# Turning the normalised rows of a fused attention and gated-MLP block: from DMA transposes to a layout in DRAM and VectorE transposes

## The chip, the cores and the metric

The kernel runs on one core of a Trainium2 chip. The metric is device time in microseconds (us) of one execution; three unprofiled runs of the kernel before gave 310.79, 310.81 and 311.08. One further execution was profiled, and the profile and the trace are from that one.

The core's engines each work through their own list of instructions in order: TensorE (PE in the profile; its weight loads are PEld), VectorE (DVE), ScalarE (ACT), GpSimd (POOL), and SyncE (SP), which here does nothing but issue DMAs. An instruction that waits holds up everything behind it on its engine. DMAs issued by SP run on 16 DMA engines.

## The reference: what is computed

```python
x = A_x                                   # 1 x 2048 x 640, bf16
xn = _layernorm(x)
return x + _A_ref(xn, A_wqkv, A_wo) + _B_ref(xn, B_w_gate, B_w_up, B_w_down)

def _A_ref(x, wqkv, wo):                  # 32 heads of 20, window 256
    q, k, v = (x @ wqkv)...               # reshaped to heads
    scores = q k^T * 20 ** -0.5           # causal, only the last 256 keys
    return softmax(scores) v @ wo

def _B_ref(x, w_gate, w_up, w_down):      # 640 -> 1536 -> 640
    return (sigmoid(x @ w_gate) * (x @ w_up)) @ w_down
```

## The kernel before

**Chunks and stages.** The 2048 rows are cut into four chunks (0 to 3) of 512 rows, four blocks of 128 rows each. Every product needs the normalised rows turned, features on the partitions: the tile `xnT[c]` (128 partitions, 5 feature groups, 512 rows). A chunk goes through these stages:

- normalising (`g_norms`, L366): for each block the statistics (`ln_block`: two BN_STATS and one aggregate on VectorE), then 1/sqrt of the variance for all four blocks on GpSimd (`rstd_blocks`, L284), then subtract and multiply on VectorE (`norm_block`, L290, tile `xn`), then the turn (`turn_block`, L302): a DMA transpose from SBUF to SBUF on SP's queue, `xn` into `xnT[c]`. Chunk 0 is turned by TensorE instead (`transpose_rows`, L296).
- `g_qk` (L391): ten products for queries and keys. Each is copied from PSUM into a staging tile `st` (six buffers; VectorE copies the queries at L323, ScalarE the keys at L325) and stored to a scratch tensor in DRAM, `sq` or `sk` (L327). From there `spread` (L329) loads the tiles `qT` and `kT` with heads of 20 padded to 32 rows. The pad rows are cleared once by DMA (`clear`, L196). The scratch exists twice, for even and odd chunks; the second pair is cleared by `clear_next`.
- `g_v` (L410): the values; each block gives two products `pv`, copied to the tile `v` by VectorE and ScalarE in turn (L358).
- `g_gu` (L432): gate and up products `pg`, `pu`; ScalarE takes tanh of `pg` (L439), and VectorE multiplies it with `pu` into `h` (L447). This `h` is 12 tiles per chunk.
- `scores` (L505) and `pv` (L531): scores of one step into `ps`, the exponential on ScalarE (`pT`, L517), masks on GpSimd (L524) or, for the steps called late, one mask on VectorE (L529), then `acc`. VectorE transposes `acc` to `t` (L555) and divides (`rec` L563, `on` L567, `oc` L571).
- `g_out` (L488): `y` from `h` and `wd` (L457) and from `oc` and `wo` (L464), the residual rows added by VectorE (L468) and the store.

`pqk`, `pv`, `pg`, `pu`, `acc` and `y` share four PSUM accumulators (pool `ps_d`): a product starts only when the copy out of the tile that had its accumulator is done.

**What sets the order.** The order is written out. The attention steps of all chunks stand in one list (`todo`). Between them the planner `Fill` (L574) draws products from a list of parts (L712 to L730), as many nanoseconds of them as a step leaves free; the cost of a part is fixed in the code. `mix(a, b, first, every, rest)` (L618) weaves two generators: after the piece of `a` with number `first`, and after every `every`-th from there, one piece of `b` follows. That is how the normalising of the next chunk gets in among the products of the current one: chunk 1 among the gate and up products of chunk 0 (`gu0a`, `gu0b`), chunk 2 in the output of chunk 0 (`out0`), chunk 3 in `gu1b` and `out1`. Loads are parts of cost 0.

**SP's queue** takes, after the parts for chunk 0: the transposes of chunk 1, the rows of chunk 2 (L159), the rearranging of the output weights from DRAM to DRAM (`turn_wo`, L229, tensor `wo_i`, eight transfers), `wd` (L225), the two pad clears (L198), four query stores, the output weights out of `wo_i` (`load_wo`, L235), and the rest of the stores and spreads. SP uses eight semaphores in turn for its DMAs, so a DMA is issued only when the one eight places earlier has landed.

## Time and profile before

| | |
|---|---|
| median of 3 unprofiled runs | 310.81 us (310.79 to 311.08) |
| profiled execution | 312.31 us |
| its span, first to last instruction | 310.5 us |
| granted TensorE clock | 1.0 |
| DMA | 35.67 MB in 40459 packets, 10560 of them under 512 B |
| transposes by DMA (L303) | 12, SP busy 1.2 us with one (median 1.22) |
| normalising, one block of 128x640 (L292) | 12, mean 640 ns |
| statistics, one half block (L272) | 28, mean 472 ns |
| VectorE transpose 128x512 bf16 (L571) | 20, mean 711 ns |

How to read the profile: a group of instructions has its line, engine, operation and tiles (out<-in), a count, and busy time. A line of the timeline starts with its start and its length in us, and ends, in brackets, with how long the engine had been idle before it and what ended that. In the list of waits, "A <- B: 2.0, 1, 2.0" is: A's engine waited for B, in total us, times, longest us. The chain that ended last is followed back from the last instruction through what released each step. "SPq" is SP issuing DMAs; when a DMA has landed is told by its semaphore in the trace.

### The profile page before, as it was taken

The page shows a single profiled execution, that of the slowest core. Times are in us where ns is not written, and L with a number is a line of the kernel's source. Part 1 is how long each engine was busy: PE and PEld are TensorE (multiplying, and loading weights), DVE is VectorE, ACT ScalarE, POOL GpSimd, SP SyncE. Part 2 cuts the span into 40 slices and gives each one's busy share as a digit, 9 for nine tenths or more (in the row PEclk, how much of TensorE's full clock was granted, in tenths as well). Part 3 has the DMA queues.
Part 4 walks back from the last instruction along what each step waited for, and adds up shares of the span by engine and source line. Part 5 has one row for each costly group of instructions (what it writes and reads, how often), then busy time and mean ns, then how long its engine had stood idle before and what let it go on. Part 6 is the DMA issues. An engine that isn't in the chain of part 4 may idle for free.

```text
span 310.5 us, 10034 instructions
## 1 busy us (share of the span) xinstructions
PE 302.4 (97%) x4343; PEld 168.1 (54%) x4343; DVE 172.0 (55%) x342; ACT 198.4 (64%) x196; POOL 165.3 (53%) x304
## 2 busy tenths in 40 slices
PE   6999999998999999999989999999999999999996
PEld 3654444544657654554556665454546665444774
DVE  5633684828697464496945346373643626372533
ACT  6923868668964648888654548978675647778000
POOL 3020668457885828566661836747383756657000
PEclk9999999999999999999999999999999999999999
DMA  7997984985705453440013512640000210000201
GB/s 206 365 327 237 330 155 150 344 260 165 231 0 89 108 158 121 155 160 2 3 23 88 87 56 89 211 155 1 4 0 4 67 40 23 2 2 2 87 23 63
DMA packets 40459, 35.67 MB, mean 115 GB/s; under 512 B 10560, under 2 KB 39872, under 8 KB 40384
## 3 DMA queue, kind: packets, MB, share of 16 engines
q1 hardware_dynamic: 39552, 34.27, 37.2%
q10 hardware_dynamic: 864, 0.77, 0.9%
q8 instruction: 34, 0.56, 0.8%
q14 instruction: 9, 0.07, 0.1%
HBM read 23.63 MB, written 10.26 MB: 109 GB/s over the span
## 4 chain that ended last, share of the span: by engine, by line
PE 90%; DVE 4%; DMA 2%; ACT 2%; issue 1%; SPq 0%; DVEq 0%; ACTq 0%
PE y L457 17%; PE pu L443 17%; PE pg L436 16%; PE pqk L319 12%; PE ps L512 8%; PE pv L349 7%; PE y L464 7%; PE acc L543 6%; DMA sq<-st 1%; ACT pT L517 1%; DVE on L567 1%; DMA xc<-in_A_x_dram 1%; DVE st L323 1%; DVE xn L292 1%; DVE h L447 0%
## 5 line engine op out<-in xcount | busy, mean ns | idle before, releaser
L524 POOL TENSOR_SCALAR_AFFINE_SELECT pT<-pT 64x512 bf16<-64x512 bf16 (+1 forms) x252 | 153.6, 609 | 103.6 <-ACT pT L517 91.8
L517 ACT ACTIVATE pT<-ps 128x2048 bf16<-128x2048 f32 x75 | 140.8, 1877 | 60.4 <-PE ps L512 57.5
L447 DVE SCALAR_TENSOR_TENSOR h<-th,pu 128x512 bf16<-128x512 f32 x48 | 32.8, 683 | 54.3 <-PE pu L443 41.7
L443 PE MATMUL pu<-xnT,wu 128*128 128x512 bf16 x240 | 59.8, 380 | 0.0
L436 PE MATMUL pg<-xnT,wg 128*128 128x512 bf16 x240 | 59.8, 380 | 0.0
L457 PE MATMUL y<-wd,h 128*128 128x320 bf16 (+2 forms) x396 | 56.8, 295 | 0.8 <-DVE h L447 0.8
L319 PE MATMUL pqk<-xnT,wqkv 128*128 128x512 bf16 x200 | 46.0, 381 | 0.0
L457 PEld LDWEIGHTS <-h 128*128 128x128 bf16 x396 | 36.6, 98 | 17.0 <-issue 2.2
L439 ACT ACTIVATE th<-pg 128x512 f32<-128x512 f32 x48 | 28.6, 596 | 15.3 <-PE pg L436 15.1
L436 PEld LDWEIGHTS <-wg 128*128 128x128 bf16 x240 | 22.3, 98 | 25.6 <-issue 2.0
L443 PEld LDWEIGHTS <-wu 128*128 128x128 bf16 x240 | 22.1, 98 | 25.4 <-issue 1.8
L319 PEld LDWEIGHTS <-wqkv 128*128 128x128 bf16 x200 | 22.6, 119 | 18.8 <-issue 1.4
L512 PE MATMUL ps<-qT,kT 20*64 20x320 bf16 (+4 forms) x1456 | 32.2, 259 | 0.3 <-issue 0.2
L512 PEld LDWEIGHTS <-kT 20*64 20x64 bf16 x1456 | 15.9, 103 | 24.8 <-issue 21.8
L555 DVE STREAM_TRANSPOSE t<-acc 128x512 f32<-128x512 f32 x32 | 21.1, 696 | 13.3 <-PE acc L543 13.3
L567 DVE TENSOR_TENSOR on<-t,rec 128x320 bf16<-128x320 f32 (+4 forms) x48 | 27.7, 576 | 1.1
L468 DVE SCALAR_TENSOR_TENSOR rows<-y,rows 128x320 bf16<-128x320 f32 x30 | 14.4, 488 | 23.8 <-PE y L464 23.5
L349 PE MATMUL pv<-wqkv,xnT 128*128 128x320 bf16 x160 | 25.9, 300 | 0.0
L464 PE MATMUL y<-wo,oc 128*128 128x320 bf16 (+2 forms) x165 | 24.2, 295 | 0.0
L543 PE MATMUL acc<-pT,v 64*32 64x320 bf16 (+4 forms) x1456 | 19.8, 252 | 1.4 <-DVE pT L529 1.4
L358 DVE CAST v<-pv 64x320 bf16<-64x320 f32 x29 | 14.1, 487 | 12.2 <-PE pv L349 11.9
L543 PEld LDWEIGHTS <-v 64*32 64x32 bf16 x1456 | 16.3, 91 | 7.4 <-issue 2.6
(48 smaller groups left out, 157.3 us busy)
## 6 DMA issues: line engine op xcount, KB each, us to landing
qT<-sq SPq DMA_DIRECT2D x16, 256.0 KB
kT<-sk SPq DMA_DIRECT2D x16, 256.0 KB
sq<-st SPq DMA_DIRECT2D x20, 128.0 KB
sk<-st SPq DMA_DIRECT2D x20, 128.0 KB
out_dram<-rows SPq DMA_DIRECT2D x15, 160.0 KB
wg<-in_B_w_gate_dram SPq DMA_DIRECT2D x4, 480.0 KB
wu<-in_B_w_up_dram SPq DMA_DIRECT2D x4, 480.0 KB
xc<-in_A_x_dram SPq DMA_DIRECT2D x3, 640.0 KB
```

The costliest lines, as they stand in the source:

```text
L319: nc.tensor.matmul(ps, lhsT=wt[:, m, :], rhs=xnT[c][:, d, :], start=(d == 0), stop=(d == DC - 1))
L349: nc.tensor.matmul(ps[:, 0:HALF], lhsT=xnT[c][:, d, s * P:(s + 1) * P], rhs=wqkv[:, d, 2 * D + hf * HALF:2 * D + (hf + 1) * HALF], start=( ...
L436: nc.tensor.matmul(pg, lhsT=part(wg, d, f), rhs=xnT[c][:, d, :], start=(d == 0), stop=(d == DC - 1))
L443: nc.tensor.matmul(pu, lhsT=part(wu, d, f), rhs=xnT[c][:, d, :], start=(d == 0), stop=(d == DC - 1))
L447: nc.vector.scalar_tensor_tensor(out=h, in0=th, scalar=1.0, in1=pu, op0=ADD, op1=MULT)
L457: nc.tensor.matmul(y[:, 0:cut[1] - cut[0]], lhsT=ht[c, f][:, s * P:(s + 1) * P], rhs=wd[:, f, cut[0]:cut[1]], start=(f == 0), stop=False)
L464: nc.tensor.matmul(y[:, 0:cut[1] - cut[0]], lhsT=oc[c, m][:, s * P:(s + 1) * P], rhs=wo[:, m, cut[0]:cut[1]], start=False, stop=(m == DC - 1))
L512: nc.tensor.matmul(ps[a * U:(a + 1) * U, i, col * U:(col + n) * U], lhsT=qk["k", kc, o // GH][32 * i:32 * i + DH, o % GH + a, kb * U:(kb + ...
L517: nc.scalar.activation(out=pt[:, :, 0:CW], in_=ps, func=EXP, scale=SCALE)
L524: nc.gpsimd.affine_select(out=view, in_=view, pattern=[[0, HG], [0, n], [sign, U]], compare_op=GE, fill=0.0, base=base, channel_multiplier ...
L543: nc.tensor.matmul(acc[32 * i:32 * i + 32, q * U:(q + n) * U], lhsT=vt[kb][a * U:(a + 1) * U, u, h * VW:h * VW + 32], rhs=pt[a * U:(a + 1) ...
L567: nc.vector.tensor_tensor(out=on[m][:, :, slot:slot + n], in0=t1[:, :, first:first + n], in1=rec.to_broadcast([P, 16, n]), op=MULT)
```

## The change

The rows of chunks 1 to 3 are no longer transposed by DMA. Each normalised block is stored to DRAM (`store_rows`, tensor `xr`, two of them). When all four blocks are stored, four loads (`load_quarters`) bring the chunk back so that quadrant q of 32 partitions holds columns 160q to 160q+159, and row t of each group of 32 rows lies on partition t; the tile is the one that held the raw rows (`xc`, one buffer). VectorE then transposes 32x32 blocks of it into `xnT[c]`, one instruction of 128x640 for a block of rows. Feature 5p+b thereby lands on partition p in group b, where before it was feature 128b+p on partition p; so `wqkv`, `wg` and `wu` are loaded by the same order, and chunk 0's TensorE transposes read every fifth column.

The statistics of chunk 1 start three pieces earlier in `gu0a`; those of chunk 2 move from `out0` into `v1` and those of chunk 3 from `gu1b` into `v2`; a number of empty pieces (`wait`) lies between the loads of the quarters and the transposes. The scratch tensors exist once and are cleared once. `turn_wo` is two transfers where it was eight, `load_wo` moves ahead of the rows of chunk 2, and these go behind `wd`.

```diff
-    wqkv_r = A_wqkv.rearrange("(c p) n -> p c n", p=P)
+    def by_feature(w):
+        return w.rearrange("(p b) n -> p b n", b=DC)
+    wqkv_r = by_feature(A_wqkv)
...
-    scratch = {(w, k): tc.dram_tile([H * 32, CW], BF16, name=f"s{w}{k}")
-               for w in "qk" for k in range(2)}
+    scratch = {w: tc.dram_tile([H * 32, CW], BF16, name=f"s{w}") for w in "qk"}
+    xn_rows = [tc.dram_tile([CW, D], BF16, name=f"xr{k}") for k in range(2)]
...
     def turn_wo():
-        for i in range(HG):
-            for a in range(2):
-                nc.sync.dma_start(out=wo_i[i].rearrange("(b a d) n -> a b d n", a=2, d=DH)[a],
-                                  in_=A_wo.rearrange("(a b i d) n -> i a b d n", a=2, i=HG, d=DH)[i, a])
+        for a in range(2):
+            nc.sync.dma_start(out=wo_i.rearrange("i (b a d) n -> a b i (d n)", a=2, d=DH)[a],
+                              in_=A_wo.rearrange("(a b i d) n -> a b i (d n)", a=2, i=HG, d=DH)[a])
...
     def transpose_rows(s, copy, lo=0, hi=DC):
+        xn = xns[0, s].rearrange("p (f b) -> p b f", b=DC)
         for d in range(lo, hi):
-            nc.tensor.transpose(pt[:, d, :], xns[0, s][:, d * P:(d + 1) * P], ident)
+            nc.tensor.transpose(pt[:, d, :], xn[:, d], ident)
...
+    def store_rows(c, s):
+        nc.sync.dma_start(out=xn_rows[c % 2][s * P:(s + 1) * P, :], in_=xns.pop((c, s)))
+    def load_quarters(c):
+        t = xp.tile([P, SBC, D], BF16, name="xc")
+        xc[c] = t
+        for q in range(4):
+            nc.sync.dma_start(out=t[32 * q:32 * q + 32].rearrange("p s (j e) -> p (s j) e", e=QF),
+                              in_=xn_rows[c % 2][:, q * QF:(q + 1) * QF].rearrange("(j t) e -> t j e", t=32))
     def turn_block(c, s):
-        nc.sync.dma_start(out=xnT[c][:, :, s * P:(s + 1) * P], in_=xns.pop((c, s)), transpose=True)
+        nc.vector.transpose(out=xnT[c][:, :, s * P:(s + 1) * P],
+                            in_=xc[c][:, s, :].rearrange("p (j f b) -> p b j f", j=SBC, b=DC))
...
         for s in range(SBC):
             norm_block(c, s, mvs[:, s, :], rstds[:, s:s + 1])
+            store_rows(c, s)
+            if s < SBC - 1:
+                yield 0
+        load_quarters(c)
+        for _ in range(wait):
             yield 0
-            if turn:
-                turn_block(c, s)
+        new_xnT(c)
+        for s in range(SBC):
+            turn_block(c, s)
+            yield 0
...
-    fill.add("gu0a", mix(g_gu(0, 0, 4), norms1, 4, 1, False), 4 * GU)
-    fill.add("gu0b", mix(g_gu(0, 4, 12), norms1, 0), 8 * GU)
-    fill.add("x2", later(load_x, 2), 0)
+    norms = {c: g_norms(c, wait) for c, wait in ((1, 8), (2, 7), (3, 7))}
+    fill.add("gu0a", mix(g_gu(0, 0, 4), norms[1], 1, 1, False), 4 * GU)
+    fill.add("gu0b", mix(g_gu(0, 4, 12), norms[1], 0), 8 * GU)
     fill.add("wo_i", later(turn_wo), 0)
     fill.add("wd", later(load_wd), 0)
-    fill.add("pads", later(clear_next), 0)
+    fill.add("wo", later(load_wo), 0)
+    fill.add("x2", later(load_x, 2), 0)
     fill.add("qk1", g_qk(1), 50 * MM)
-    fill.add("v1", mix(g_v(1), g_gu(1, 0, 2), 1, 2), 40 * 136 + 2 * GU)
-    fill.add("out0", mix(g_out(0, g_gu(1, 2, 3)), norms2, 1, 1), OUT + GU)
+    fill.add("v1", mix(mix(g_v(1), g_gu(1, 0, 2), 1, 2), norms[2], 2, 1, False), 40 * 136 + 2 * GU)
+    fill.add("out0", mix(g_out(0, g_gu(1, 2, 3)), norms[2], 1, 1), OUT + GU)
     fill.add("x3", later(load_x, 3), 0)
     fill.add("qk2", g_qk(2), 50 * MM)
-    fill.add("v2", mix(g_v(2), g_gu(1, 3, 7), 0, 1), 40 * 136 + 4 * GU)
-    fill.add("gu1b", mix(g_gu(1, 7, 12), norms3, 0, 1, False), 5 * GU)
-    fill.add("out1", mix(g_out(1, g_gu(2, 0, 1)), itertools.chain(norms3, g_turns(3)), 1, 3), OUT + GU)
+    fill.add("v2", mix(mix(g_v(2), g_gu(1, 3, 7), 0, 1), norms[3], 8, 1, False), 40 * 136 + 4 * GU)
+    fill.add("gu1b", mix(g_gu(1, 7, 12), norms[3], 0, 1, False), 5 * GU)
+    fill.add("out1", mix(g_out(1, g_gu(2, 0, 1)), norms[3], 1, 1), OUT + GU)
```

More of the change, by code (lines that the diff above doesn't have):

```diff
@@ L27 @@
 FS = 768
+QF = D // 4
 EPS = 1e-5
@@ L189, with clear @@
     load_wqkv(1)
-    scratch = {(w, k): tc.dram_tile([H * 32, CW], BF16, name=f"s{w}{k}")
-               for w in "qk" for k in range(2)}
+    scratch = {w: tc.dram_tile([H * 32, CW], BF16, name=f"s{w}") for w in "qk"}
+    xn_rows = [tc.dram_tile([CW, D], BF16, name=f"xr{k}") for k in range(2)]
     zero = kp.tile([P, GH, CW], BF16, name="kT")
     nc.gpsimd.memset(zero[:, 0:3, :], 0.0)
-    def clear(w, k):
-        rows = scratch[w, k].rearrange("(h j) s -> h (j s)", j=32)[:, DH * CW:]
+    def clear(w):
+        rows = scratch[w].rearrange("(h j) s -> h (j s)", j=32)[:, DH * CW:]
         nc.sync.dma_start(out=rows.rearrange("h (a e) -> h a e", a=4), in_=zero[:, 0:3, :])
@@ L201, in load_gu @@
         nc.sync.dma_start(out=t[k][:, :, lo:hi],
-                          in_=w.rearrange("(c p) f -> p c f", p=P)[:, :, k * FS + lo:k * FS + hi])
+                          in_=by_feature(w)[:, :, k * FS + lo:k * FS + hi])
     load_gu(wg, B_w_gate, 0, 0, FS // 2)
     load_gu(wu, B_w_up, 0, 0, FS // 2)
-    clear("q", 0)
-    clear("k", 0)
+    clear("q")
+    clear("k")
     load_gu(wg, B_w_gate, 0, FS // 2)
@@ L216, in load_rest @@
         spread("k", 0, 4, NG)
-    def clear_next():
-        clear("q", 1)
-        clear("k", 1)
     def load_wd():
@@ L325, in proj_block @@
             nc.scalar.copy(out=st, in_=ps)
-        dst = scratch[w, c % 2].rearrange("(h j) s -> h j s", j=32)
+        dst = scratch[w].rearrange("(h j) s -> h j s", j=32)
         nc.sync.dma_start(out=dst[:, 4 * m:4 * m + 4, :], in_=st)
@@ L333, in spread @@
             qk[w, c, half] = (qp if w == "q" else kp).tile([P, GH, CW], BF16, name=w + "T")
-        src = scratch[w, c % 2].rearrange("(a b p) s -> b p a s", a=2, p=P)
+        src = scratch[w].rearrange("(a b p) s -> b p a s", a=2, p=P)
         for b in range(g0 // 2, g1 // 2):
@@ L364, with g_norms @@
     MM = 216
-    def g_norms(c, turn, behind=0):
-        new_xnT(c)
+    def g_norms(c, wait):
         mvs = lnp.tile([P, SBC, nc.vector.BN_AGGR_DIM], FP32, name="mvs", bufs=1)
@@ L374, in g_norms @@
                 yield 0
-        for _ in range(behind):
-            yield 0
         rstds = rstd_blocks(mvs)
@@ L381, in g_norms @@
             norm_block(c, s, mvs[:, s, :], rstds[:, s:s + 1])
+            store_rows(c, s)
[3 more added lines that the diff above has]
+        for _ in range(wait):
             yield 0
-            if turn:
-                turn_block(c, s)
-    def g_turns(c):
+        new_xnT(c)
         for s in range(SBC):
@@ L398, in g_qk @@
                     load_gu(wu, B_w_up, 0, FS // 2)
-                if c == 1 and w == "q" and m == 3:
-                    load_wo()
                 if c and w == "k" and m == 1:
@@ L707, in later @@
         yield 0
-    norms1 = g_norms(1, True)
-    norms2 = g_norms(2, True, 1)
-    norms3 = g_norms(3, False)
-    fill.add("gu0a", mix(g_gu(0, 0, 4), norms1, 4, 1, False), 4 * GU)
-    fill.add("gu0b", mix(g_gu(0, 4, 12), norms1, 0), 8 * GU)
-    fill.add("x2", later(load_x, 2), 0)
+    norms = {c: g_norms(c, wait) for c, wait in ((1, 8), (2, 7), (3, 7))}
+    fill.add("gu0a", mix(g_gu(0, 0, 4), norms[1], 1, 1, False), 4 * GU)
+    fill.add("gu0b", mix(g_gu(0, 4, 12), norms[1], 0), 8 * GU)
     fill.add("wo_i", later(turn_wo), 0)
     fill.add("wd", later(load_wd), 0)
-    fill.add("pads", later(clear_next), 0)
+    fill.add("wo", later(load_wo), 0)
+    fill.add("x2", later(load_x, 2), 0)
     fill.add("qk1", g_qk(1), 50 * MM)
-    fill.add("v1", mix(g_v(1), g_gu(1, 0, 2), 1, 2), 40 * 136 + 2 * GU)
-    fill.add("out0", mix(g_out(0, g_gu(1, 2, 3)), norms2, 1, 1), OUT + GU)
+    fill.add("v1", mix(mix(g_v(1), g_gu(1, 0, 2), 1, 2), norms[2], 2, 1, False), 40 * 136 + 2 * GU)
+    fill.add("out0", mix(g_out(0, g_gu(1, 2, 3)), norms[2], 1, 1), OUT + GU)
     fill.add("x3", later(load_x, 3), 0)
     fill.add("qk2", g_qk(2), 50 * MM)
-    fill.add("v2", mix(g_v(2), g_gu(1, 3, 7), 0, 1), 40 * 136 + 4 * GU)
-    fill.add("gu1b", mix(g_gu(1, 7, 12), norms3, 0, 1, False), 5 * GU)
-    fill.add("out1", mix(g_out(1, g_gu(2, 0, 1)), itertools.chain(norms3, g_turns(3)), 1, 3), OUT + GU)
+    fill.add("v2", mix(mix(g_v(2), g_gu(1, 3, 7), 0, 1), norms[3], 8, 1, False), 40 * 136 + 4 * GU)
+    fill.add("gu1b", mix(g_gu(1, 7, 12), norms[3], 0, 1, False), 5 * GU)
+    fill.add("out1", mix(g_out(1, g_gu(2, 0, 1)), norms[3], 1, 1), OUT + GU)
     fill.add("qk3", g_qk(3), 50 * MM)
```

## The prediction

> **What bounds the kernel now.** I read the engine totals first, then the chain that ended last, then the waits.

> ```profile
> PE 302.4 (97%) x4343; PEld 168.1 (54%) x4343; DVE 172.0 (55%) x342; ACT 198.4 (64%) x196; POOL 165.3 (53%) x304
> ...
> PE 90%; DVE 4%; DMA 2%; ACT 2%; issue 1%; SPq 0%; DVEq 0%; ACTq 0%
> ```

> TensorE (PE) is busy 302.4 of 310.5 us and 90% of the chain is its own work. The order of its instructions, and ScalarE's, is the same in the changed program as built. So the change can only remove idle time of TensorE or add some. The table of 10 us stretches puts the idle at the start (2.4 us up to 10 us), at the end (3.6), and in between at 60-80 us (0.57 + 0.87), 150-160 (0.84) and some 0.3 more. The last three, about 2.6 us, are all that a better order could win. Who waits there, from the list of waits:

> ```profile
> ACT st L325 <- DMA sq<-st: 2.0, 1, 2.0
> ...
> PE acc L543 <- DVE pT L529: 1.4, 1, 1.4
> ...
> PE y L457 <- DVE h L447: 0.8, 1, 0.8
> ```

> The first two are one event, at 69.4-70.9 us; the chain in order of time shows it:

> ```profile
> 63.68 4.43 DMA sq<-st
> 68.14 1.90 ACT pT L517
> 70.14 0.69 DVE pT L529
> ```

> ScalarE may not overwrite a staging tile until its store to DRAM has landed. The first query store of chunk 1 was issued at 60.02 and landed at 67.02 (the trace's landings): on most DMA engines by 63.1, on four of them 3.9 us later. Those four still had the rearranging of the output weights (wo_i, L232): eight transfers of 4 rows of 25.6 KB, each landing on 4 engines. The DMA share while little else ran says so too:

> ```profile
> 51.00:52.00 1.00, 1.00 (x7) 0.43 (x5) 0.00 (x0) 1.00 (x2) 0.91 (x2) 1.00 0.19 77
> 52.00:53.00 1.00, 1.00 (x6) 0.45 (x5) 0.39 (x1) 0.57 (x2) 0.78 (x2) 1.00 0.27 111
> ```

> The two last columns, DMA share and GB/s: a fifth to a quarter is 4 of 16 engines.

> **The change, part by part**, in the clock of before.

> *Removed*: 12 DMA transposes (SP is busy 1.2 us with each) and the second pair of pad clears (2 x 384 KB). *Added*: 12 row stores (128 packets of 1280 B), 12 quarter loads (512 packets of 320 B) and 12 VectorE (DVE) transposes of 128x640. Row for the last: oc<-on, 128x512 bf16, 711 ns, so 711 x 640/512 = 0.89 us; strided reading by it is not shown, so 0.7 to 1.2. Row for the packets: the trace's records have 18 ns at 256 B, 24 at 384 and 46 at 1024, so about 21 ns for 320 B; one quarter load is 32 packets on each engine, 0.67 us (0.58 to 1.5 by those ends). *Moved*: statistics and normalising of chunks 1 to 3 go earlier on VectorE, and an in-order queue makes everything behind them later.

> (a) *Chunk 1, 27-71 us.* The four statistics blocks (1.0 us each: 2 x 0.47 + 0.21, pipelined) fall into VectorE's idle time at 27-33; the row stores are out at 36.6 to 40.2, the last lands at about 43.6 behind the loads still queued, and the quarter loads, which SP issues only then, land by 48.4. The first transpose stands behind the h that ended at 50.7: 2.3 us of cover. Four of them end near 55.1, with 0.2-0.3 us for the first query product at 54.96 to wait. That wait is swallowed by the next one, whose end is set by DMAs. On the four engines: before, the x load landed at 50.9, wo_i took to 59.9, wd 5.0 more, the clears 1.9, the first query store 0.3. After, wo_i's rows start behind the quarter loads (48.4, 2.5 us earlier) and still lead with a dimension of 4, so I keep 4 engines; behind wd stand wo (four loads, 0.82 each, 3.3), now issued ahead of the query stores as SP waits there for wo_i, and the x load of chunk 2 (1.7). The sum is -2.5 + 3.3 + 1.7 - 1.9 = **+0.6 us**; ends: -1.4 (the stall gone) and +2. The x load lands at about 66 and is needed at 76.5, wo is needed at 90: covered.

> (b) *Value projection of chunk 1, 76-84 us.* Here nothing hides the statistics.

> ```profile
> 75.90 0.58 DVE L567 TENSOR_TENSOR on<-t,rec 128x320 bf16<-128x320 f32 x1
> ...
> 76.51 0.99 DVE L358 CAST v<-pv 64x320 bf16<-64x320 f32 x2
> ...
> 77.53 0.69 DVE L447 SCALAR_TENSOR_TENSOR h<-th,pu 128x512 bf16<-128x512 f32 x1
> ...
> 78.20 0.99 DVE L358 CAST v<-pv 64x320 bf16<-64x320 f32 x2
> ...
> 81.10 0.99 DVE L358 CAST v<-pv 64x320 bf16<-64x320 f32 x2 [1.91 <-PE pv L349]
> ...
> 81.58 1.24 PE L443 MATMUL pu<-xnT,wu 128*128 128x512 bf16 x5
> ```

> The changed order puts four blocks among the first four: block, cast, block, block, h, block, cast. From 76.48 that is 4 x 1.0 + 0.98 + 0.69 + 0.98, so the second cast ends at 83.1, not 79.2. TensorE has four accumulators for all this; in the changed program pu at 81.6 waits for that cast's, so it starts at 83.2: **+1.55 us** (1.0 to 2.0).

> (c) *Output of chunk 0, 90-98 us.* VectorE's backlog pushes the last normalised block to 92.0 (84.1 + two xn 1.1, h 0.7, two transposes 1.3, xn 0.5, the old run of 3.7 us from 85.05 to 88.77, xn 0.5). Its store lands 2.0 us after issue (the output store issued at 94.15 landed at 96.20), the first quarter load 2.6 after that (kT<-sk: issued 75.89, landed 78.50), the others 0.67 apart: 98.7. The first transpose waits for that, and in VectorE's queue the masking that TensorE needs is behind it:

> ```profile
> 95.19 0.43 DVE L529 TENSOR_TENSOR pT<-pT,edge 128x512 bf16<-128x512 bf16 x1 [1.07 <-ACT pT L517]
> ...
> 95.61 1.29 PE L543 MATMUL acc<-pT,v 64*32 64x320 bf16 x96
> ```

> The mask ends at 98.75 + 0.89 + 0.43 = 100.1. TensorE, 1.55 late, needs it two thirds into acc, at 95.61 + 1.55 + 0.8 = 98.0: **+2.1 us** (1.0 to 3.5).

> (d) *Value projection of chunk 2, 137-144 us.* Three blocks now precede the h of 138.19, with no idle time ahead:

> ```profile
> 137.22 0.93 DVE L567 TENSOR_TENSOR on<-t,rec 128x320 bf16<-128x320 f32 x1
> ...
> 138.19 0.69 DVE L447 SCALAR_TENSOR_TENSOR h<-th,pu 128x512 bf16<-128x512 f32 x1
> ...
> 139.64 1.24 PE L443 MATMUL pu<-xnT,wu 128*128 128x512 bf16 x5
> ```

> h ends at 138.15 + 3.0 + 0.69 = 141.85; pu waits for its accumulator and starts at 141.9: **+2.25 us** (1.5 to 2.7). The fourth block, a cast and four xn follow while TensorE has work, and cost nothing more.

> (e) *155-158 us.* The two xn (1.59 us) ahead of h at 156.81 are gone and the four transposes stand behind it, before 4 us of idle VectorE: the wait of 0.84 goes, **-0.84** (0 if h is late otherwise; next late there is nothing).

> *At nothing*: weights by other rows (as many packets of 640 to 1280 B, two-sided 0.3 at the start); the 20 transposing weight loads of chunk 0, which now read with a step of 5 (119 ns where L319 does so, 98 without: at most 0.4, mostly beside VectorE's work); the residual rows of chunk 0, loaded behind the row stores on SP, land near 91 and are needed at 93.

> Sum: 0.6 + 1.55 + 2.1 + 2.25 - 0.84 = **5.7 us**. The profiled execution took 312.31, its span of 310.5 and 1.8 around it; that makes 318.0. It is 1.5 us over the median of the unprofiled runs, 310.81, so I predict **316.5 us**; with the parts' ends 314 to 320.

> **Rivals.**

> *VectorE absorbs it* (0.10). It is 55% busy and the added transposes are 10.7 us of 310. If no matmul waits longer, both stalls go: 310.8 - 1.44 - 0.84 = **308.5**. It decides at the cover in (b) and (d): 2.4 us (79.2 to 81.6) and 0.75 (138.9 to 139.64), so a block of at most 0.25 us. For it: the average. Against: blocks take 1.0 in this trace.

> *wo_i on 16 engines* (0.15). If a transfer of 4x4 rows is spread by rows, each engine moves 2 rows, not 8; the queue is 5.7 us shorter and the stall at 69 goes: -1.44 instead of +0.6, **314.5**. Against it: the leading 4 went to 4 engines before. [...]

> *Small packets cost like large ones* (0.12). At the 46 ns of a 1 KB packet a quarter load takes 1.5 us and four of them 3.3 us more: +3.3 in (a), +2.5 in (c), **322.3**. Against it: the 24 ns at 384 B. [...]

> **How the numbers follow.** Forecast 0.60, rivals 0.10, 0.15 and 0.12, the rest 0.03. The range takes in the second and third rival with their spread and leaves out the first: 312.5 to 322.5. 0.2% (0.6 us) is about what a measurement of this kernel can tell from no change. Faster 0.11, same 0.02, slower 0.87.

> **What would show it.** Right: a wait of pu for VectorE of 1 to 2 us near 82 and 2 to 3 near 143; acc waiting for the mask near 101, itself behind a wait for xc<-xr; the wait of y for h gone; a stall near 71 that still ends with a query store. Wrong: statistics that delay no pu, quarter loads that land before VectorE asks, or query stores landing before 65.

## The result and the profile after

| | before | after |
|---|---|---|
| median of the runs on one chip | 310.80 us (310.58 to 311.08, 4 runs) | 328.81 us (327.55 to 330.02, 4 runs) |
| ratio, 95% interval | | 1.058 (1.054 to 1.062) |
| profiled execution, its span | 312.31, 310.5 | 328.61, 326.4 |
| mean granted TensorE clock in the span | 1.0 | 0.979 |

The change costs 18.0 us, not the 5.7 of the forecast's 316.5; 328.81 lies outside the range of 312.5 to 322.5. The page of the changed kernel: engine totals, the granted clock in 40 slices of 8.2 us, and the chain.

```profile
PE 305.6 (94%) x4308; PEld 170.3 (52%) x4343; DVE 181.3 (56%) x354; ACT 198.5 (61%) x196; POOL 165.8 (51%) x304
...
PEclk9999999996999599999999999999999999999999
...
PE 73%; DMA 12%; DVE 6%; SPq 3%; ACT 2%; issue 2%; POOL 1%; DVEq 0%; ACTq 0%
```

The chain is 73% TensorE's own work where it was 90%, with 12% of DMA in place of 2%. The clock has two dips, at about 74 to 82 and 106 to 114 us, which the page of before does not have. The waits of the changed kernel:

```profile
ACT st L339 <- DMA sq<-st: 6.8, 1, 6.8
DVE xnT L316 <- DMA xc<-xr: 6.7, 1, 6.7
...
PE acc L554 <- DVE pT L540: 5.1, 2, 4.0
...
PE acc L554 <- ACT st L339: 4.0, 1, 4.0
...
PE pu L454 <- DVE h L458: 2.2, 1, 2.2
```

Three waits stand where the prediction put them: ScalarE on a query store, acc on the mask behind the quarter loads, pu on h. The first costs TensorE 5.05 us where 2.0 were forecast (1.44 and the 0.6 of (a)), the second 4.0 where 2.1 were. The wait of pu for VectorE near 82 us, forecast at 1 to 2 us, is only 0.4 long.

TensorE's order is the same in both programs, so equal matmuls can be matched and the start of one subtracted from the other: that gives the delay at each point. For before I use a second profile of it (`before_again`, below), whose own time is typical. The steps of the delay, by the prediction's letters:

| stretch (clock of before) | forecast | measured | of it waiting | of it half clock |
|---|---|---|---|---|
| up to 66 us | 0 to 0.3 | +0.4 | 0.4 | 0 |
| (a) chunk 1, 66 to 74 | +0.6 | +7.2 | 4.6 | 2.6 |
| (b) value projection of chunk 1 | +1.55 | +0.6 | 0.6 | 0 |
| (c) output of chunk 0, 94 to 102 | +2.1 | +6.8 | 4.0 | 2.8 |
| (d) value projection of chunk 2 | +2.25 | +2.3 | 2.2 | 0 |
| (e) 155 to 158 | -0.84 | -0.5 | | |
| rest, near 205 | 0 | +0.6 | | |

The sum is 17.4 of a difference of spans of 17.2 (326.4 less 309.2). (a)'s waiting is 3.96 + 1.09 less 0.5 that before has there. The half-clock column is an estimate: in the changed kernel's trace one matmul of 128x320 followed another every 267 ns at half clock (`y` at 109 us) and every 136 ns at full clock (116 us), so I let a stretch at half clock lose half of the time in which TensorE works. In (c) it is 6.83 us long, and TensorE stands for 1.16 of it: (6.83 - 1.16) / 2 = 2.8; the same way (6.83 - 1.65) / 2 = 2.6 in (a).

(a) in stretches of 1 us. The columns are the busy times of PE, PEld, DVE, ACT and POOL with their counts, then the granted clock, the DMA share and GB/s.

```profile
68.00:69.00 1.00, 1.00 (x5) 0.35 (x3) 0.00 (x0) 0.00 (x0) 0.00 (x0) 1.00 0.92 263
69.00:70.00 1.00, 0.09 (x1) 0.00 (x0) 0.00 (x0) 0.00 (x0) 0.00 (x0) 1.00 0.65 196
...
72.00:73.00 1.00, 0.00 (x0) 0.00 (x0) 0.00 (x0) 0.59 (x2) 0.00 (x0) 0.76 0.26 89
73.00:74.00 1.00, 0.93 (x28) 0.58 (x36) 0.00 (x0) 1.00 (x2) 0.00 (x0) 0.50 0.08 27
```

The five engines stand from 69.1 to 72.4 while only DMAs run; then the clock is 0.50, and it stays so until 79.4 though TensorE works again. The same in (c), in stretches of 2 us:

```profile
102.00:104.00 2.00, 1.83 (x72) 1.27 (x70) 0.00 (x0) 0.47 (x1) 0.34 (x1) 1.00 0.85 175
104.00:106.00 2.00, 0.00 (x0) 0.00 (x0) 0.00 (x0) 0.00 (x0) 0.00 (x0) 1.00 1.05 249
106.00:108.00 2.00, 0.17 (x9) 0.15 (x16) 1.41 (x3) 0.00 (x0) 0.00 (x0) 0.66 0.04 15
108.00:110.00 2.00, 2.00 (x59) 1.21 (x44) 1.77 (x3) 0.48 (x1) 0.00 (x0) 0.50 0.04 8
...
114.00:116.00 2.00, 2.00 (x37) 1.30 (x36) 1.66 (x5) 1.03 (x1) 0.60 (x1) 1.00 0.30 87
```

What stood ahead of both waits, from the chain of the changed kernel in order of time:

```profile
48.39 10.68 DMA wo_i<-in_A_wo_dram
59.53 9.10 DMA wo<-wo_i
68.69 4.67 DMA sq<-st
...
102.70 3.76 DMA xc<-xr
106.59 0.88 DVE xnT L316
107.83 0.95 PE acc L554 x32
```

In (a) the rearranging, then the wo loads, then the stores: one queue. In (c) a quarter load, one transpose, and acc. VectorE's timeline shows what stands in its queue there:

```profile
97.97 0.55 DVE L293 TENSOR_SCALAR xn<-xc,mvs,rstds 128x640 bf16<-128x640 bf16 x1
...
106.59 0.88 DVE L316 STREAM_TRANSPOSE xnT<-xc 128x640 bf16<-128x640 bf16 x1 [6.67 <-DMA xc<-xr]
107.39 0.38 DVE L540 TENSOR_TENSOR pT<-pT,edge 128x512 bf16<-128x512 bf16 x1
```

The last normalised block ends at 98.5, its store lands at 100.3, the four quarter loads by 106.5: 7.9 us later, and for 6.67 of them VectorE stands, with a mask of 0.38 us behind the transpose.

### The profile page after: what moved, and what is told of

It is laid out like the page before. It is cut to its first block, busy times and chain, and to the rows that moved or that the text cites. A ratio compares the mean times of both kernels' runs of the same rounds, so it can differ in the third digit from the quotient of the medians.

```text
span 326.4 us, 10015 instructions
## 1 busy us (share of the span) xinstructions
PE 305.6 (94%) x4308; PEld 170.3 (52%) x4343; DVE 181.3 (56%) x354; ACT 198.5 (61%) x196; POOL 165.8 (51%) x304
## 4 chain that ended last, share of the span: by engine, by line
PE 73%; DMA 12%; DVE 6%; SPq 3%; ACT 2%; issue 2%; POOL 1%; DVEq 0%; ACTq 0%
PE y L468 15%; PE pu L454 13%; PE pg L447 13%; PE pqk L333 10%; PE y L475 7%; PE ps L523 6%; PE pv L363 5%; PE acc L554 5%; DMA wo_i<-in_A_wo_dram 3%; DMA wo<-wo_i 3%; DMA xr<-xn 2%; ACT pT L528 2%; DMA wqkv<-in_A_wqkv_dram 2%; SPq L312 1%; DMA sq<-st 1%
## 5 line engine op out<-in xcount | busy, mean ns | idle before, releaser
L454 PE MATMUL pu<-xnT,wu 128*128 128x512 bf16 x230 | 58.9, 380 | 3.3 <-DVE h L458 2.2
L447 PE MATMUL pg<-xnT,wg 128*128 128x512 bf16 x225 | 58.5, 380 | 1.1 <-issue 0.5
L333 PE MATMUL pqk<-xnT,wqkv 128*128 128x512 bf16 x190 | 45.1, 381 | 0.8 <-issue 0.4
L447 PEld LDWEIGHTS <-wg 128*128 128x128 bf16 x240 | 22.2, 98 | 25.6 <-issue 2.0
L554 PE MATMUL acc<-pT,v 64*32 64x320 bf16 (+4 forms) x1456 | 21.6, 260 | 9.1 <-DVE pT L540 5.1
L479 DVE SCALAR_TENSOR_TENSOR rows<-y,rows 128x320 bf16<-128x320 f32 x30 | 14.6, 489 | 25.9 <-PE y L475 25.6
L363 PE MATMUL pv<-wqkv,xnT 128*128 128x320 bf16 x160 | 26.8, 309 | 0.5 <-DMA wqkv<-in_A_wqkv_dram 0.5
L578 DVE TENSOR_TENSOR on<-t,rec 128x320 bf16<-128x320 f32 (+4 forms) x48 | 26.6, 555 | 1.1
L475 PE MATMUL y<-wo,oc 128*128 128x320 bf16 (+2 forms) x165 | 25.6, 306 | 0.0
L554 PEld LDWEIGHTS <-v 64*32 64x32 bf16 x1456 | 17.0, 93 | 16.0 <-issue 6.9
L363 PEld LDWEIGHTS <-xnT 128*128 128x128 bf16 x160 | 15.0, 100 | 9.9 <-issue 1.4
```

Source lines behind the costliest of these rows:

```text
L333: nc.tensor.matmul(ps, lhsT=wt[:, m, :], rhs=xnT[c][:, d, :], start=(d == 0), stop=(d == DC - 1))
L363: nc.tensor.matmul(ps[:, 0:HALF], lhsT=xnT[c][:, d, s * P:(s + 1) * P], rhs=wqkv[:, d, 2 * D + hf * HALF:2 * D + (hf + 1) * HALF], start=( ...
L447: nc.tensor.matmul(pg, lhsT=part(wg, d, f), rhs=xnT[c][:, d, :], start=(d == 0), stop=(d == DC - 1))
L454: nc.tensor.matmul(pu, lhsT=part(wu, d, f), rhs=xnT[c][:, d, :], start=(d == 0), stop=(d == DC - 1))
L475: nc.tensor.matmul(y[:, 0:cut[1] - cut[0]], lhsT=oc[c, m][:, s * P:(s + 1) * P], rhs=wo[:, m, cut[0]:cut[1]], start=False, stop=(m == DC - 1))
L554: nc.tensor.matmul(acc[32 * i:32 * i + 32, q * U:(q + n) * U], lhsT=vt[kb][a * U:(a + 1) * U, u, h * VW:h * VW + 32], rhs=pt[a * U:(a + 1) ...
```

## The experiments

All are timed against before on the same chip, and the ratios compare those runs. The table gives each, with the delay of TensorE over before (second profile) at the ends of the parts.

| kernel | us (median) | before, us | ratio (95%) | after (a) | after (b) | after (c) | after (d), (e) |
|---|---|---|---|---|---|---|---|
| after | 328.81 | 310.80 | 1.058 (1.054-1.062) | 7.6 | 8.3 | 15.1 | 16.9 |
| wo_back | 321.46 | 311.3 | 1.032 (1.029-1.035) | 0.2 | 1.8 | 7.0 | 10.4 |
| wo_x2_back | 324.32 | 311.3 | 1.041 (1.037-1.044) | -0.3 | 3.8 | 10.2 | 13.5 |
| wo16 | 326.38 | 311.3 | 1.048 (1.044-1.053) | 7.5 | 7.5 | 13.5 | 16.8 |
| stats3_later | 326.39 | 311.3 | 1.048 (1.045-1.051) | 9.2 | 9.2 | 14.9 | 15.3 |
| c_wait | 314.82 | 311.7 | 1.010 (1.007-1.012) | 0.3 | 1.9 | 1.9 | 3.7 |
| combo2 | 313.06 | 311.7 | 1.006 (1.004-1.008) | 0.3 | 1.9 | 1.9 | 1.9 |
| b22 | 313.33 | 311.7 | 1.004 (1.002-1.007) | -0.4 | 0.9 | 0.9 | 0.9 |
| b33 | 312.58 | 311.7 | 1.004 (1.002-1.006) | -0.3 | 0.5 | 0.5 | 0.5 |
| before_wo16 | 311.82 | 311.6 | 1.001 (0.999-1.002) | -0.4 | 0.3 | 0.3 | 0.3 |
| b33_wo16 | 312.48 | 311.6 | 1.003 (1.001-1.005) | 0.0 | 1.1 | 1.1 | 1.1 |
| after_again | 329.84 | 311.5 | 1.057 (1.053-1.061) | 8.4 | 8.4 | 14.7 | 18.0 |
| keep_busy | 329.53 | 311.5 | 1.055 (1.050-1.059) | 9.7 | 10.4 | 14.1 | 17.5 |
| c_wait_alone | 323.06 | 311.5 | 1.035 (1.031-1.039) | 7.9 | 8.1 | 8.1 | 9.9 |

**before_again**: before, unchanged.

> The kernel before, unchanged, for a second profile of it. Its first profiled execution took 312.31 us, 1.5 over the median of the others (310.81). Theory: that execution had lost about 1.5 us somewhere that this one shows (a stall that is shorter here), so that the delays counted against its trace are too small by that much: a span of about 309 and a time of about 310.8. Rival: the time is 310.8 with the same span of 310.5, the loss lies outside the span.

The median was 311.08, the profiled execution 311.03 with a span of 309.2. In the list of TensorE's waits the two stalls of the prediction are 0.5 and 0.4, where the first profile had 1.4 and 0.8:

```profile
PE acc L543 <- DVE pT L529: 0.5, 1, 0.5
PE y L457 <- DVE h L447: 0.4, 1, 0.4
```

So the theory held: the execution profiled first was 1.5 us above the others because of those two stalls. Of the 2.3 us that the prediction counted as winnable there, a usual run has 0.9.

**wo_back**: the wo loads back behind the fourth query block.

```diff
-    fill.add("wo", later(load_wo), 0)
...
+                if c == 1 and w == "q" and m == 3:
+                    load_wo()
```

> One part undone: the four loads of the output weights (wo<-wo_i) are issued where the kernel before had them, behind the fourth query block of chunk 1, not ahead of all query stores. The changed kernel took 328.8 us; its first query store landed at 72.25 us and TensorE stood idle 69.1 to 73.0 and 75.0 to 76.1, then ran at half clock until 79.4. Theory A (the store is late because on four DMA engines it stands behind the rearranging, wd, wo and the x load of chunk 2): without wo's 3.6 us ahead of it the first query store lands at about 68.6, the idle time at 69 falls to about 1.3 us, the clock is not halved, and the time falls by 5 to 6 us, to about 323.3. Theory B (the store is late because SyncE issues it late, at 65.0 instead of 60.0, held by the wait of the wo loads for the rearranging and by the x load; the queue on the engines matters little): the store is issued at about 60.5 and lands at about 67.5, the time is about 322.5. Rival C (stores are late for the quarter loads and the transposes of VectorE, which make the projection of chunk 1 later): nothing changes, 328.8.

It took 321.46, 1.8 less than theory A said and 1.0 less than B. The store was issued at 58.28 (after: 65.00) and landed at 66.29 (after: 72.25). Both theories hold part of it: the store is issued 6.7 us earlier, and what stands ahead of it in the queue still counts, with 8.0 us from issue to landing (after: 7.25). And wd, which followed the rearranging by 7.6 us in the changed kernel (59.07 to 66.65), follows it here by 5.0 (59.21 to 64.20): the wo loads ahead of the stores had also slowed wd. In the packet records the 1280-byte packets of that time (61 to 63 us) take 133 to 144 ns in the changed kernel, 55 here. Rival C is out. The idle time at 69 is gone. Where the clock is concerned, this run shows something new, at (d), in stretches of 2 us:

```profile
146.00:148.00 2.00, 0.00 (x0) 0.00 (x0) 1.90 (x7) 1.34 (x4) 0.17 (x1) 1.00 0.00 0
148.00:150.00 2.00, 1.98 (x13) 0.64 (x20) 1.89 (x6) 0.00 (x0) 0.75 (x2) 0.64 0.03 8
150.00:152.00 2.00, 2.00 (x20) 0.58 (x5) 1.75 (x3) 1.53 (x1) 1.90 (x6) 0.51 0.00 0
```

The same wait of pu of 2.2 us that cost 2.3 in the changed kernel is followed by half clock here, from 148.56 to 151.97, and costs 3.9.

**wo_x2_back**: the x load of chunk 2 moved behind the projection too.

```diff
-    fill.add("x2", later(load_x, 2), 0)
     fill.add("qk1", g_qk(1), 50 * MM)
+    fill.add("x2", later(load_x, 2), 0)
```

> As wo_back, and the x load of chunk 2 too is issued behind the projection of chunk 1 (after its ten blocks), so that only the rearranging and wd stand ahead of the query stores. Theory A: the first query store lands 1.6 us earlier than in wo_back, at about 67.0 as in the kernel before, the idle time at 69 is that of before or less (1.4), time about 322.8; the x load lands at about 74 and is needed at about 76, so no new wait. Theory B: as wo_back, 322.5, without a further gain. Rival C: 328.8. If the x load of chunk 2 comes too late for the statistics, a new wait of VectorE for it near 77 and a time above wo_back's.

The first store landed 1.3 us earlier, at 64.99, but the x load landed at 78.77, not 74, since it was issued only at 74.15. VectorE's list of waits has a new one, and (b) costs 4.1 us in place of 1.6:

```profile
DVE stats L273 <- DMA xc<-in_A_x_dram: 3.8, 1, 3.8
```

**wo16**: the rearranging on 16 engines.

```diff
+        def pieces(w):
+            return w.rearrange("b (e f) -> e b f", e=16)
-        for a in range(2):
-            nc.sync.dma_start(out=wo_i.rearrange("i (b a d) n -> a b i (d n)", a=2, d=DH)[a], ...
+        for i in range(HG):
+            for a in range(2):
+                nc.sync.dma_start(out=pieces(wo_i[i].rearrange("(b a d) n -> a b (d n)", a=2, d=DH)[a]), ...
```

> Only the rearranging of the output weights is changed against the changed kernel: eight transfers whose slowest dimension is 16 pieces of 1600 B of each 25.6 KB row block, in place of two transfers whose slowest dimension is 4. Order of all queues as in the changed kernel. Theory A: all 16 engines share it, it lands within about 3 us of its last issue (by 54 instead of 59), nothing on four engines is late, the first query store lands by 64 and the idle time at 69 goes entirely; the clock stays full: 328.8 - 6.0 = 322.8, or a little less. Rival (the four engines are not the cause; the queue as a whole is full in 50 to 70): landing and time stay within 1 us of 328.8. Extra issues on SyncE, six of 0.6 us, cost nothing by either.

It landed on all 16 engines, at 57.19 in place of 59.07, but the first query store landed at 71.20, only 1.0 us earlier, and its first engine at 68.20, where the changed kernel's first engine had it at 68.36. So theory A was wrong in its "four engines": with wd, wo and the x load ahead of it the store is late on every engine. What fits these landings is that everything ahead in the queue counts. The rival's time, within 1 us of 328.8, fits the profiled execution (328.18) but not the median, 326.38, which is 2.4 lower; where that went was not found.

**stats3_later**: the statistics of chunk 3 begin in gu1b.

```diff
-    fill.add("v2", mix(mix(g_v(2), g_gu(1, 3, 7), 0, 1), norms[3], 8, 1, False), 40 * 136 + 4 * GU)
+    fill.add("v2", mix(g_v(2), g_gu(1, 3, 7), 0, 1), 40 * 136 + 4 * GU)
```

> One part undone: the statistics and normalising of chunk 3 begin in the gated part of chunk 1 that follows (gu1b), not inside the value projection of chunk 2; nothing else differs from the changed kernel. There pu waited 2.2 us for VectorE at 153.9 to 156.1, behind three blocks of statistics. Theory: that wait goes and nothing takes its place, 328.8 - 2.3 = 326.5. Rival: VectorE has the same work a little later, the wait of y for h (0.84 in the kernel before) comes back near 172 and the transposes of chunk 3 are late for its projection: 327.5 to 329.

The wait of pu is gone, and the delay does not grow at (d) at all. But the rival's wait is back as well:

```profile
PE y L468 <- DVE h L458: 0.8, 1, 0.8
```

So (e) costs 0.5 here, where the changed kernel wins 0.5. That the median, 326.39, meets the theory's 326.5 is in part luck: by the traces 2.3 us go at (d), 1.0 comes back at (e), and (a) and (c), which this edit does not touch, differ by 1.8 and 1.2 in opposite directions from one execution to the other.

**c_wait**: wo_back, and 11 steps of waiting for chunk 2.

```diff
-    norms = {c: g_norms(c, wait) for c, wait in ((1, 8), (2, 7), (3, 7))}
+    norms = {c: g_norms(c, wait) for c, wait in ((1, 8), (2, 11), (3, 7))}
```

> On top of wo_back (321.5 us), one number: chunk 2 waits 11 steps instead of 7 between its quarter loads and its transposes, so that VectorE's queue holds the mask and the two transposes of the accumulators ahead of the first transpose of rows. In wo_back acc waited 3.6 us for the mask (97.4 to 101.0), behind a wait of 6.4 us for the quarter loads, and TensorE ran at half clock from 100.8 to 104.2. Theory (the stall is the mask standing behind the wait for the quarter loads): the wait of 3.6 goes, and the half-clock window of 3.4 us with its loss of up to 1.7 us goes with it: 321.5 - 5.2 = 316.3. Rival 1 (the idle time alone counts, the clock follows by itself elsewhere): 321.5 - 3.6 = 317.9. Rival 2 (VectorE's backlog or the quarter loads delay the output of chunk 0 anyway, the additions behind the transposes are late instead): above 319.

314.82, 1.5 less than the theory. The delay does not grow at (c), where it grew by 5.2 in wo_back, and at (d) it grows by 2.3 in place of 3.9, since no half-clock stretch follows there in this run. VectorE's timeline has the mask ahead, and the first transpose without a wait:

```profile
96.13 0.42 DVE L542 TENSOR_TENSOR pT<-pT,edge 128x512 bf16<-128x512 bf16 x1 [2.70 <-ACT pT L530]
...
103.39 0.89 DVE L316 STREAM_TRANSPOSE xnT<-xc 128x640 bf16<-128x640 bf16 x1
```

**combo2, b22, b33**: the parts put together.

```diff
 combo2: c_wait and stats3_later
 b22:    combo2, but ..., norms[2], 2, 2, False) in v1, and (2, 9)
 b33:    combo2, but ..., norms[2], 3, 3, False) in v1, and (2, 9)
```

> c_wait, and the statistics of chunk 3 begin in gu1b as in stats3_later. In wo_back the wait of pu for VectorE (2.2 us at 146 to 148) was followed by half clock from 148.6 to 152.0; against the kernel before the delay grew by 2.9 us there. Theory: against c_wait another 2.9 us go, 313.4; what is left over the kernel before is the value projection of chunk 1 (+1.6 us of waits for VectorE behind the statistics of chunk 2) and about 1 us. Rival: only the wait of 2.3 less the 1.0 that the changed order wins at the gated part of chunk 1 goes, 315.

> combo2, with the statistics of chunk 2 at every second step of the value projection of chunk 1 instead of every step (one block, a cast, one block, h, a cast, two blocks), and 9 steps of waiting for the quarter loads. Theory (b: pu at 81.6 waits because three blocks stand ahead of the second cast): the +1.6 us there goes, 313.4 - 1.6 = 311.8, or with the stall of 1.4 at 69 that the kernel before had gone too, 310 to 311. Rival (the four blocks cost the same anywhere in the projection): as combo2. Rival 2 (the normalised rows now come about 4 us later, and the quarter loads are too late for the transposes): a wait of VectorE for xc<-xr with the additions behind it, and a time of 314 or more.

> As b22, with the statistics of chunk 2 at every third step (always one block between two casts, the fourth block in the output of chunk 0), so that VectorE is never held for more than one block, and the normalised rows come later still, the last just ahead of the mask. Theory: as b22 or up to 0.3 us less in the projection, but the last normalised block is at about 96 and the quarter loads land near 105, transposes from 106 on against a first use near 109.6 in the clock of the kernel before: 310 to 312. Rival: the mask or the projection of chunk 2 is late, 313 or more.

313.06, 313.33 and 312.58. combo2 met its 313.4 by two misses that cancel: against c_wait 1.8 us went and not 2.9, since c_wait had no half clock at (d) to lose, and c_wait itself had come out 1.5 below its theory. In b22 and b33 the traces show (b) shrink from 1.6 to 1.3 and 0.8 us, but the three times cannot be told apart: their intervals in the table overlap. Neither came to the 310 to 311 hoped for: the stall at 69 that I meant to win is 0.5 in a usual run of before, and this line of TensorE's timeline in b33 is new:

```profile
79.39 0.43 PE L525 MATMUL ps<-qT,kT 20*64 20x320 bf16 x24 [0.73 <-DMA kT<-sk]
```

**before_wo16 and b33_wo16**: the edit of wo16 on before and on b33.

> The kernel before with the rearranging of the output weights alone changed as in wo16: each of its eight transfers in 16 pieces of 1600 B a row block, on 16 engines in place of four. The kernel before waits 1.44 us at 69.4 for a query store that landed on four engines 3.9 us after the others. In wo16 this did not help (1 us), since wd and the loads that the change puts ahead of the stores fill all engines; here only wd and the pad clears stand ahead. Theory: the rearranging lands by 56 instead of 59.9, the query store by 64, the stall of 1.44 us goes: 310.8 - 1.4 = 309.4, faster than both kernels. Rival (the queue as a whole is the bound here too): 310.8, no difference.

> b33 (312.6 us) with the rearranging on 16 engines. In b33 the query stores of chunk 1 no longer hold anything, so the rearranging has cover on four engines. Theory: no difference, 312.6. Rival (six more issues of SyncE push the wd loads and the query stores back by 3 us, or wd lands earlier and its queue clears): 1 us up or down.

In before the query store then lands at 63.98 as the theory said (unchanged it landed between 63.14 and 64.81 on twelve engines and between 65.75 and 67.02 on four, so the 3.9 us of the prediction are from the first engine to the last), and the time is the same, 311.82 against 311.61: the stall goes, but the trace has 0.7 us more at 79. The rival was right on the time. b33_wo16 is b33. No kernel tried here beats before.

**after_again, keep_busy, c_wait_alone**: the price of the clock, and whether the parts add up. keep_busy, whose matmuls are never read:

```diff
         for k, (pt, j, q, n, col) in enumerate(flat):
+            if (c, o, k) == (1, 0, 8):
+                ps = ps_s.tile([P, HG, CW], FP32, name="ps")
+                for r in range(16):
+                    nc.tensor.matmul(ps[:, r % HG, :], lhsT=ident, rhs=wd[:, 0, 0:CW], start=True, stop=True)
```

> The changed kernel, unchanged, on the same chip as the next two, for their difference: 328.8 us. Its trace shows the same two idle times of about 4 us (near 70 and 104), each with a half-clock window behind it; whether the clock drops after the wait of 2.2 us near 154 depends on where that wait falls against a grid of 3.41 us, on which all drops of one run lay so far. Theory of the grid: every start of a half-clock window in this run lies a whole multiple of 3.41 us from every other, and each lasts 3.41, 6.83 or 10.24 us.

> The changed kernel with 16 matmuls of 128x512 (weights of the output MLP against the identity, results never read) put into TensorE's queue ahead of the block of acc that waits for the mask near 104, about 3.45 us of work inside a wait of 4.0. All waits stay as they are; only the idle time is filled. Theory (the price of the stall is 4.0 us of waiting and about 2.8 us more because the clock is halved 2.8 us into it, from 106.7 to 113.5): the clock stays full there, the mask comes at the same time, and the time falls by 2.3 to 2.8 us, to about 326.2. Rival (the matmuls behind the stall are slow for another reason, or there is no such price): the time is as after_again or up to 0.5 us longer.

> The changed kernel with 11 steps of waiting in place of 7 for chunk 2, nothing else: the mask stands ahead of the transposes. Theory (the parts add up): the whole of part (c) goes, its wait of 4.0 and its half-clock windows, 6.8 us by the trace: 328.8 - 6.8 = 322.0. Rival (with chunk 1 still late by 6 us, VectorE or the quarter loads are late for something else there): 324 or more.

In after_again the half-clock stretches start at 74.42, 108.55 and 156.34: 34.13 and 47.79 apart, 10 and 14 times 3.413. The wait at (d) was halved this time. Before the timeline of keep_busy (15 of its 16 matmuls have a record) stands the same place in after_again; then come two stretches of 2 us of keep_busy:

```profile
108.48 0.93 PE L554 MATMUL acc<-pT,v 64*32 64x256 bf16 x32 [4.39 <-DVE pT L540]
```

```profile
105.07 0.91 PE L558 MATMUL acc<-pT,v 64*32 64x320 bf16 x64
105.91 3.63 PE L553 MATMUL ps<-wd,ident 128*128 128x512 bf16 x15
109.46 0.58 PE L558 MATMUL acc<-pT,v 64*32 64x256 bf16 x32
```

```profile
108.00:110.00 2.00, 2.00 (x48) 0.88 (x46) 1.91 (x3) 0.00 (x0) 0.00 (x0) 1.00 0.00 0
110.00:112.00 2.00, 2.00 (x45) 1.47 (x38) 1.92 (x3) 1.40 (x1) 0.00 (x0) 1.00 0.03 8
```

The block of acc behind the filled wait takes 0.58 us in place of 0.93 to 0.95, the clock stays at 1.00, and (c) costs 3.7 us in place of 6.8 in the first profile of the changed kernel and 6.3 in after_again. Not all of the difference is the clock. In the first profile 4.0 is the wait and 2.8 the half clock; in after_again 4.4 is the wait, and the half-clock stretch of 3.41 us, in which TensorE never stands, is worth 1.7. So filling the wait wins back 1.7 to 2.8 us of half clock, and the rest is a shorter wait. As a whole the kernel is not measurably faster (329.53, its six times from 325.4 to 332.6), so on the time the rival was nearer. In its profiled execution, 332.6, the longest of the six, TensorE loses 3.0 us more near 220 with a wait that the profile puts to no other engine ("issue"), and 0.8 more at (a) than after_again. So the verdict is on the stretch, not on the total. c_wait_alone took 323.06, between the theory's 322.0 and the rival's 324. In its trace (c) adds nothing (8.1 before it and behind it), so the cause of (c) holds. That its median lies 6.8 us below that of after_again, the figure of the theory, is in part luck: (c) cost 6.3 in after_again's trace, and the two profiled executions lie 9.2 apart, with 1.6 of it at (d), which is halved in after_again and not here, and 1.1 near 205.

## Why the prediction was wrong, point by point

**(a) failed, by the most.** The step was "-2.5 + 3.3 + 1.7 - 1.9 = +0.6 us". Its terms for wo, the x load and the clears were right: 3.6, 1.6 and the clears gone. The other two were not. The rearranging was to end 2.5 us earlier, having started behind quarter loads that land by 48.4; these landed at 50.60, only 0.3 before the x load that stood there in before (50.90), and the rearranging ended at 59.07, 0.8 earlier than the 59.87 of before. And wd behind it was taken at 5.0 as before; it took 7.6, with the wo loads running beside it. Together -0.8 + 7.6 - 5.0 + 3.6 + 1.6 - 1.9 = +5.1, and the store landed 5.2 later. wo_back shows that one placement, the wo loads ahead of the query stores, is the cause of nearly all of (a): without it the delay there is 0.2 in place of 7.6, and 7.4 us of time go. That the store must be late on four engines only, as the prediction read it in before, does not hold for the changed kernel: there the first engine had it at 68.36 (63.14 in before), twelve by 69.18 and the last four by 72.25, and with the rearranging on 16 engines it is nearly as late (wo16).

**(c) was the right mechanism, under-sized.** The mask stood behind a transpose that waited for the quarter loads, as forecast; c_wait and c_wait_alone show it by moving the transpose alone. The wait was 4.0, not 2.1: against TensorE's progress the last normalised block came 0.7 us later than worked out, and store and quarter loads took 7.9 us from it, not 6.7: the first quarter load landed 3.75 us behind the store (104.07 against 100.32) instead of 2.6, and the others up to 0.93 apart instead of 0.67.

**What the sum did not have at all is the clock.** It added waits as if the work behind them cost the same, and so put the clock at nothing. The two waits of 4 us were followed by 6.83 us each at clock 0.50: 2.6 and 2.8 us. With those and the two mis-sized waits, the forecast's 5.7 becomes 5.7 + 4.0 + 1.9 + 5.4 = 17.0; the small misses (-0.9 at (b), and 0.3, 0.4 and 0.6 at (e), up to 66 us and near 205) add 0.4 to that. keep_busy shows that it is TensorE's standing that brings the half clock at (c): filled, the clock stays at 1.00. The profile of before shows no drop inside the span (clock 1.0), and its longest wait there was 1.44 us. In the trace of the changed kernel the clock is 1.0 or 0.5 and nothing between, and its two half-clock stretches, of 6.83 us each, start at 72.52 and 106.66: 34.13 apart, as the first two of after_again. The prediction should have asked of each wait whether it brings that price.

**(d) and (e) were right in their mechanism**: 2.3 against 2.25 (stats3_later and combo2 show it), and the wait of y for h is gone. (e) is worth 0.5 and not 0.84, as a usual run of before has only 0.4 of that wait. The forecast also took 1.5 us off for the profiled execution; before_again shows that this is what the two stalls had beyond a usual run, 0.9 at (a) and 0.5 at (e), so the 0.5 was counted twice. **(b)** was 0.6 in the changed kernel and 1.6 in wo_back, c_wait and combo2 against 1.55: right where chunk 1 is not already late. Between the two stands the half-clock stretch of (a), in which VectorE catches up; that is argued from the order of events, not shown by itself.

**The rivals.** "wo_i on 16 engines" did not arise (its 25.6 KB packets ran on four engines again, 0.96 us each in the median); made to arise in wo16, it moved the query store by only 1.0 us. "Small packets cost like large ones" is out: 320-byte packets took 21 to 26 ns on average in the 1-us stretches of (c), 25 to 29 over a whole run, and 43 at most in any 1-us stretch of any run with 20 packets or more, not 46. "VectorE absorbs it" is out by the waits above.

**What the change is worth with its three misplacements mended** (b33): 0.4% over before (0.2 to 0.6). So the new path for the rows is nearly free; the 18 us are the order around it. What is left of it by the trace (0.5 us near 79, 0.5 near 205, less 0.2 won between) was not taken apart further.

## What to carry to other kernels

Before moving a load on a shared DMA queue, list the stores behind it that free a buffer, and count in full what then stands ahead of them (the wo loads ahead of the query stores: 7.4 us); and put nothing behind a wait for a round trip through DRAM in an in-order queue that another engine needs sooner (here 7.9 us from the last normalised block to the last quarter load, with a mask behind it). Price a wait of TensorE by its length and by what follows: the 2.2 us of standing at (d) cost 2.3 in the changed kernel, where the clock stayed full, and 3.9 in wo_back, where 3.41 us at half clock followed. Take a second profile of the baseline before counting a stall of 1 us as winnable (1.4 and 0.5 us in two profiles of before).
